# An order of instructions planned by the kernel itself, up to attention's end

## The chip, the cores and the metric

The kernel runs on one core of a Trainium2 chip. The metric is the device time of one execution in microseconds (us); less is better. Five engines each work through a list of instructions in order: PE (matrix products, into PSUM), ACT (functions of one operand), DVE and POOL (elementwise work and reductions) and SP, which here only issues transfers. An instruction waits by semaphores for what it needs, and everything behind it on the same engine waits with it.

## The reference

Attention with normalised queries and keys, then two feed-forward layers over the 1792 tokens. All numbers are float32; the weights come as 64-bit floats, whose two halves the kernel loads and joins itself.

```python
batch, n_heads, seq, head_dim = (4, 12, 448, 64)
q_n, k_n = (rmsnorm(q, g_q), rmsnorm(k, g_k))
scores = scale * np.matmul(q_n, k_n.transpose(0, 1, 3, 2))
scores = scores - np.max(scores, axis=-1, keepdims=True)
attn = np.exp(scores)
attn = attn / (np.sum(attn, axis=-1, keepdims=True) + 1e-09)
x = np.matmul(attn, v)            # then [1792, 768]
h = x @ w_in                      # 768 -> 1024
solu = h * softmax(h)
ln = (solu - mu) / np.sqrt(var + 1e-06) * g_ln
y = ln @ w_out                    # 1024 -> 768
h2 = y @ w2_in                    # 768 -> 2048
out = (h2 - np.tanh(h2)) @ w2_out
```

## The kernel before

Attention runs over 24 pairs of heads, six to a batch. For a pair `load_qk` and `load_v` fetch the data, `norm` scales q and k (squares on ACT, sums `ss` and the root `rr` on DVE and ACT, the product `qn` on POOL), and `qk_trans` transposes them on PE (`qkps`, L276). A matrix is kept as a rounded part and the rest, `wk` and `wq`, which SP copies into one of three large buffers K and Q (`k<-wk`, `q<-wq`). Each pair has two heads, and each head is one "tile" here, 48 in all.

For each tile PE first forms scores for the maxima of the rows (`mps`, L342 and L350), which DVE reduces (`nm`, L351). Four columns of them are transposed (`nmps`, L358), ACT copies the result (`nt`, L360), and SP sends these 2 KB into Q (`q<-nt`, L363), so that the maxima are subtracted by the product itself. Then come the scores (`sps`, L386; for the first pair L380 to L383), their exponential on ACT (`pf`, L395), the product with v (`pvps`, L409), which also gives the sums, and their reading (`sx` and `xu`, L426 and L427). `x_norm` divides (`xo`) and SP stores the result (`xd<-xo`). `mps` and `sps` share three PSUM buffers (`ps_x`), each of which is free when DVE or ACT has read it; `pvps` has two, everything else three (`ps_m`).

The first feed-forward layer runs over blocks of tokens: four blocks of 384, the last with 256 more. As soon as attention has finished a block's tokens, `stage` works on it while later pairs run: `x_split` loads the result back (`xr<-xd`, L504) and splits it on ACT and DVE (`xs`, L195 and L196), `moe_h` multiplies (`hps`), `layer_norm` works on DVE and ACT, `moe_lnT` transposes (`lps`), `moe_x2` multiplies (`x2ps`). Class `Stream` loads weights (`raw`), joins their halves (`val`, L135 to L147), splits them (`w`) and stores them for later blocks (`w_in<-w`, `w_out<-w`). After attention the last block and the second layer (`h2ps`, `ops`) follow.

What is written first is set by two things in the source: a list of attention's steps, sorted by slot (`at`, `step`, `LAG`), of which `attn_next` writes one, and `overlap`, which writes so many of these between the pieces of `stage` as their estimated costs say. The language's own scheduler then places all instructions of the whole program: it simulates the program with its own costs and gives each engine its list, taking what was written earlier first among what its simulation finds ready. SP's list of transfers comes from it too.

Of the kernel before, what the change touches and what calls it, by code (L numbers as in the profile page):

```python
# [8 lines left out]
F32 = mybir.dt.float32  # L9
# [4 lines left out]
AX = mybir.AxisListType  # L14
PSUM = bass.MemoryType.PSUM


@with_exitstack
def kernel(
# [13 lines left out]
):  # L33
    nc = tc.nc
    B, H, S, D = q.shape
# [22 lines left out]

    const = ctx.enter_context(tc.tile_pool(name="const", bufs=1))
    raw_p = ctx.enter_context(tc.tile_pool(name="raw", bufs=2))  # L60
    dram = ctx.enter_context(tc.tile_pool(name="dram", bufs=1, space=bass.MemoryType.DRAM))

    idf = const.tile([128, 128], F32)
    mhalf = const.tile([128, 1], F32)
    eps = const.tile([128, 1], F32)
    tiny = const.tile([128, 1], F32)
    gam = const.tile([128, 1], F32)
    gam2 = const.tile([128, 1], F32)
    gln = const.tile([128, KF1], F32)
    x2d = dram.tile([128, KD, NTOK], F32)  # L70
    xd = dram.tile([128, KD, NTOK], F32)

# [406 lines left out]
    def attn_next():  # L479

        if attn_i[0] < len(attn):
            key = attn[attn_i[0]][0:2]
            while attn_i[0] < len(attn) and attn[attn_i[0]][0:2] == key:
                _, _, _, fn, args = attn[attn_i[0]]
                fn(*args)
                attn_i[0] += 1
            return key
        return (10 ** 6, 0)
# [183 lines left out]
    nc.scalar.preload_act_table_set("natural_log_exp_and_others")  # L672
    make_identity(nc, idf)
    nc.vector.memset(mhalf, -0.5)
    nc.vector.memset(eps, 1e-6)
    nc.vector.memset(tiny, 1e-9)
    ea, eb, ec, ep = ExitStack(), ExitStack(), ExitStack(), ExitStack()
    ps_m = ctx.enter_context(tc.tile_pool(name="ps_m", bufs=3, space=PSUM))
    ps_x = ep.enter_context(tc.tile_pool(name="ps_x", bufs=3, space=PSUM))
    ps_v = ep.enter_context(tc.tile_pool(name="ps_v", bufs=2, space=PSUM))  # L680
    for name, bufs in (
        ("xs", 1), ("xr", 2), ("hb", 3), ("one", 1), ("lnT", 1), ("x2", 2), ("small", 4), ("w", 5),
    ):
        Bp[name] = eb.enter_context(tc.tile_pool(name="b_" + name, bufs=bufs))
    for name, bufs in (
        ("one", 1), ("sq", 2), ("qk", 2), ("vh", 3), ("qt", 1), ("pct", 2),
        ("pc", 6), ("xu", 1), ("xo", 1), ("small", 2),
    ):
        A[name] = ea.enter_context(tc.tile_pool(name="a_" + name, bufs=bufs, side="right"))
    items, w_at = [], {}  # L690
# [9 lines left out]


    attn_next()
    ones = A["qt"].tile([128, 1], F32, tag="ones", name="ones")
# [18 lines left out]
    def overlap(b, batch):  # L722
        left = attn_left(H * (batch + 1) + 3) if batch is not None else 0
        total = stage_cost(b)
        done, spent = 0, 0.0
        for cost in stage(b):
            spent += cost
            while done < left and done < left * spent / total:
                attn_next()
                done += 1  # L730
        while done < left:
            attn_next()
            done += 1

    b = 0
    for batch in range(1, B):
# [3 lines left out]
        overlap(b, batch)  # L740
        b += 1
    ea.close()
    ep.close()
# [4 lines left out]
    def open_c(side, sizes):  # L748
        for name, bufs in sizes:
            C.setdefault(name, []).extend(  # L750
                [ec.enter_context(tc.tile_pool(name=f"c_{name}_{side}{len(C)}", bufs=bufs, side=side))] * bufs
            )

    open_c("right", (("wi", 4), ("wo", 1), ("xh0", 2), ("ob0", 1), ("g", 2), ("th", 2)))
    for name, bufs in (("xs", 1), ("lnT", 1), ("hb", 2)):
        Bp[name + "+"] = eb.enter_context(tc.tile_pool(name=f"b_{name}_2", bufs=bufs, side="right"))
    ps_h = ec.enter_context(tc.tile_pool(name="c_ps_h", bufs=5, space=PSUM))

# [120 lines left out]
```

## Time and profile before

| | |
|---|---|
| time, three runs | 1105.93 us median, 1101.46 to 1106.56 |
| profiled execution, its span from first to last instruction | 1107.5 us |
| PE busy / weight loads | 1043.3 us, 94% / 864.2 us, 78% |
| DVE, ACT, POOL busy | 690.5, 493.1, 236.4 us |
| mean granted PE clock | 0.983 |
| DMA over the span | 171.16 MB, 155 GB/s |

The profiled execution's own time is given only as its span, which lies 1.6 us above the median. Busy shares are means over a first half in which all engines work and a second one in which PE works almost alone. Matmuls are pipelined and the ends of their records are modelled, so that "busy" on PE may hold short gaps. The granted clock is the share of full speed (2.4 GHz) that PE was given; it has two levels, 1.00 and 0.50.

### The profile page before, as it was taken

What the parts mean: (1) busy time and instruction counts of PE and PEld (TensorE: products, weight loads), DVE (VectorE), ACT (ScalarE), POOL (GpSimd) and SP (SyncE); (2) the same over time, 40 slices, a digit from 0 to 9 for tenths busy, and PEclk for the clock granted to TensorE, in tenths of its full rate; (3) what the DMA queues carried; (4) which work ended last, traced back from release to release, by engine and by line L of the source; (5) the groups of instructions that cost most, each with busy time, mean ns of one, the idle gap of its engine ahead of it and who ended that gap; (6) DMA issues with size and microseconds to landing.
All of it is one profiled execution on the core that took longest, in us unless ns stands there. A gap on an engine that the chain in (4) does not pass through costs nothing.

```text
span 1107.5 us, 15169 instructions
## 1 busy us (share of the span) xinstructions
PE 1043.3 (94%) x5348; PEld 864.2 (78%) x5348; DVE 690.5 (62%) x1311; ACT 493.1 (45%) x994; POOL 236.4 (21%) x204
## 2 busy tenths in 40 slices
PE   4989999989887899999999999999999999999998
PEld 2555566648664678778889989898999989898988
DVE  8766686787787453633684066475767666675444
ACT  4667776777677455555255154311212121212110
POOL 2511123121102110001420034242414141322000
PEclk9999999989988999999999999999999999999999
DMA  7987789866996987666786443021112111110004
GB/s 182 274 227 192 179 216 281 207 181 178 284 320 185 327 229 216 192 209 203 227 291 208 138 162 95 23 74 39 57 40 59 55 58 58 57 57 1 1 29 171
DMA packets 113743, 171.16 MB, mean 155 GB/s; under 512 B 31940, under 2 KB 79492, under 8 KB 113668
## 3 DMA queue, kind: packets, MB, share of 16 engines
q1 hardware_dynamic: 112368, 170.20, 52.8%
q8 instruction: 42, 0.69, 0.3%
q14 instruction: 33, 0.27, 0.1%
q10 hardware_dynamic: 1300, 0.01, 0.1%
HBM read 109.32 MB, written 29.10 MB: 125 GB/s over the span
## 4 chain that ended last, share of the span: by engine, by line
PE 72%; DMA 15%; DVE 6%; ACT 4%; issue 1%; SPq 1%; POOL 1%; ACTq 0%; DVEq 0%; POOLq 0%
PE pvps L409 9%; PE ops L191 7%; PE ops L192 7%; PE ops L190 7%; PE h2ps L191 7%; PE h2ps L192 7%; PE h2ps L190 7%; PE sps L386 4%; DMA raw<-in_moe_w_out_dram 3%; PE x2ps L190 3%; PE x2ps L191 3%; PE x2ps L192 3%; DMA q<-nt 2%; DMA raw<-in_moe_w_in_dram 2%; DMA w<-w_in 2%; PE mps L350 1%
## 5 line engine op out<-in xcount | busy, mean ns | idle before, releaser
L820 DVE TENSOR_TENSOR ob<-ops,ob 128x384 f32<-128x384 f32 x196 | 108.5, 554 | 104.1 <-PE ops L192 103.6
L161 POOL TENSOR_TENSOR w<-val,w 128x512 fp32r<-128x512 f32 x60 | 82.5, 1377 | 424.6 <-ACT w L160 397.0
L409 PE MATMUL pvps<-pf,va 128*128 128x448 f32 (+1 forms) x384 | 164.9, 598 | 0.9 <-ACT pf L395 0.9
L191 PE MATMUL ops<-w,gT 128*128 128x384 f32 x448 | 150.6, 336 | 0.0
L190 PE MATMUL ops<-w,gT 128*128 128x384 f32 x448 | 150.3, 336 | 0.0
L192 PE MATMUL ops<-w,gT 128*128 128x384 f32 x448 | 150.2, 335 | 0.0
L351 DVE TENSOR_REDUCE nm<-mps 128x1 f32<-128x448 f32 x168 | 102.6, 617 | 71.1 <-PE mps L350 61.2
L192 PE MATMUL h2ps<-x2s,w 128*128 128x512 f32 (+1 forms) x384 | 140.9, 367 | 0.0
L386 PE MATMUL sps<-q,k 128*128 128x448 f32 (+1 forms) x368 | 118.1, 415 | 24.2 <-DMA q<-nt 9.7
L191 PE MATMUL h2ps<-x2s,w 128*128 128x512 f32 (+1 forms) x384 | 140.9, 367 | 0.0
L190 PE MATMUL h2ps<-x2s,w 128*128 128x512 f32 (+1 forms) x384 | 140.5, 366 | 0.0
L797 ACT ACTIVATE th<-h2ps 128x512 f32<-128x512 f32 (+1 forms) x64 | 34.8, 544 | 182.5 <-PE h2ps L192 182.3
L386 PEld LDWEIGHTS sps<-q,k 128*128 128x128 f32 (+1 forms) x368 | 63.0, 186 | 60.2 <-ACT pf L395 17.6
L395 ACT ACTIVATE pf<-sps 128x448 f32<-128x448 f32 x167 | 88.3, 539 | 38.5 <-PE sps L386 32.5
L409 PEld LDWEIGHTS pvps<-pf,va 128*128 128x128 f32 (+1 forms) x384 | 63.4, 202 | 42.9 <-issue 35.6
L190 PE MATMUL hps<-w,xs 128*128 128x256 f32 (+1 forms) x276 | 90.6, 329 | 2.6 <-DMA w<-w_in 2.6
L266 POOL TENSOR_TENSOR qn<-qk,rr 112x512 f32<-112x512 f32 x44 | 49.0, 1135 | 195.8 <-DVE rr L247 74.7
L350 PE MATMUL mps<-k,q 128*128 128x448 f32 (+1 forms) x144 | 78.4, 553 | 11.1 <-ACT pf L395 3.3
L191 PEld LDWEIGHTS ops<-w,gT 128*128 128x128 f32 x448 | 84.2, 188 | 4.7
L190 PEld LDWEIGHTS ops<-w,gT 128*128 128x128 f32 x448 | 84.2, 188 | 4.4
L192 PE MATMUL hps<-w,xs 128*128 128x256 f32 (+1 forms) x276 | 85.9, 313 | 0.0
L191 PE MATMUL hps<-w,xs 128*128 128x256 f32 (+1 forms) x276 | 85.7, 311 | 0.0
(118 smaller groups left out, 2042.0 us busy)
## 6 DMA issues: line engine op xcount, KB each, us to landing
w<-w_out SPq DMA_DIRECT2D x48, 512.0 KB
raw<-in_moe_w_in_dram SPq DMA_DIRECT2D x36, 512.0 KB
raw<-in_moe_w_out_dram SPq DMA_DIRECT2D x36, 512.0 KB
w<-w_in SPq DMA_DIRECT2D x24, 512.0 KB
k<-wk SPq DMA_DIRECT2D x46, 224.0 KB
q<-wq SPq DMA_DIRECT2D x46, 224.0 KB
w_in<-w SPq DMA_DIRECT2D x12, 512.0 KB
w_out<-w SPq DMA_DIRECT2D x12, 512.0 KB
```

The lines of the kernel that those rows point to most:

```text
L161: nc.gpsimd.tensor_tensor(out=w[:, 1], in0=x, in1=w[:, 0].bitcast(F32), op=ALU.subtract)
L190: nc.tensor.matmul(ps, lhsT=a[0], rhs=w[0], start=first, stop=False)
L191: nc.tensor.matmul(ps, lhsT=a[0], rhs=w[1], start=False, stop=False)
L192: nc.tensor.matmul(ps, lhsT=a[1], rhs=w[0], start=False, stop=last)
L266: eng.tensor_tensor(out=qn[:, a].rearrange("p c h d -> p h c d"), in0=t[:, a], in1=rr[:, a].rearrange("p h (c o) -> p h c o", o=1).to_broa ...
L350: nc.tensor.matmul(ps, lhsT=qh[:, f:f + 128], rhs=kh, start=True, stop=True)
L351: nc.vector.tensor_reduce(out=nm_t[p][:, c:c + 1], in_=ps, axis=AX.X, op=ALU.max, negate=True)
L386: nc.tensor.matmul(o, lhsT=K[p % NQ][:, i, z, k0:k0 + m], rhs=qcols(Q[p % NQ], slice(0, 128), p, i, z), start=(z == 0), stop=(z == 1))
L395: nc.scalar.activation(out=x, in_=ps, func=AF.Exp)
L409: nc.tensor.matmul(pv_t[n], lhsT=w, rhs=pc_t.pop((n, j))[r], start=first, stop=last)
L797: nc.scalar.activation(out=th, in_=ps, func=AF.Tanh)
L820: nc.vector.tensor_tensor(out=o, in0=ps, in1=o, op=ALU.add)
```

## The change

New classes wrap tiles (`View`, `Ref`), pools and engines. From the first step of attention to the end of the last `overlap` that holds attention steps, an instruction is not given to the language but noted, with the parts of buffers that it reads and writes. Then `plan` places them: for each engine it takes, among the noted instructions whose inputs and buffers are free by its reckoning, the one that was written first, at the earliest time; `cost` gives each a duration, `transfer` and the lines on `wire` and `lanes` a time to each DMA. A PSUM tile is opened only when the other inputs of its matmuls are there. `give` hands them out in that order, in a scope in which the language's scheduler keeps the order it gets. From there on the scheduler works as before. `rank`, `lag` and `reserve` have values with which they change no choice. Every noted instruction is issued by one line of `take`, L188, which is why the new pieces all say L188.

```diff
@@ new classes ahead of the kernel @@
+class Pool:
+    def __init__(self, rec, tiles, bufs, psum, name):
+        self.rec, self.tiles, self.bufs, self.psum, self.name = rec, tiles, bufs, psum, name
+
+    def tile(self, shape, dtype, tag=None, name=None):
+        return Ref(self.rec, self, shape, dtype, tag or name, name or tag)
+
+
+class Engine:
+    def __init__(self, rec, name, real):
+        self.rec, self.name, self.real = rec, name, real
+
+    def __getattr__(self, what):
+        f = getattr(self.real, what)
+        if not callable(f):
+            return f
+
+        def call(*a, **kw):
+            self.rec.take(self.name, what, f, a, kw)
+
+        return call
+
+
...
+    def take(self, eng, what, f, a, kw):
+        if not self.on:
+            return f(*[_real(x) for x in a], **{n: _real(x) for n, x in kw.items()})
+        op = Op()
+        op.eng = "dma" if what == "dma_start" else eng
+        op.queue, op.what, op.f, op.a, op.kw = eng, what, f, a, kw
+        op.at, op.rank = len(self.ops), self.rank
+        outs = list(a[:1]) + [kw[n] for n in ("out", "accum_out") if n in kw]
+        ins = list(a[1:]) + [x for n, x in kw.items() if n not in ("out", "accum_out")]
...
+        self.ops.append(op)
+
+    def cost(self, op):
+        n = 1
+        for d in (op.out.shape if isinstance(op.out, View) else [1, 1])[1:]:
+            n *= d
+        src = next((x for x in op.ins if isinstance(x, View)), None)
+        m = n
+        if src is not None:
+            m = 1
+            for d in src.shape[1:]:
+                m *= d
+        big = max(n, m)
+        if op.queue == "tensor":
+            if op.what == "transpose":
+                return (0.095 if n < 128 else 0.108), 0.2
+            rhs = op.kw["rhs"]
+            if rhs.root.dtype != F32:
+                return 0.0025 + n * 0.000451, 0.2
+            return (0.475 if rhs.p1 - rhs.p0 == 64 else 0.75), 0.2
+        if op.eng == "dma":
+            return 0.46, 0.0
...
+        if big <= 16:
+            return 0.18, 0.034
+        slow = isinstance(src, View) and src.dims and abs(src.dims[-1][0]) > 1
+        return 0.156 + 0.00103 * big + (0.1 if slow else 0.0), 0.034
+
+    @staticmethod
+    def transfer(op):
...
+        packets = -(-4 * size // run)
+        return max(1, packets / 16.0) * (8 + 0.05 * run) * 1e-3
+
+    def plan(self):
...
+        def can(op):
+            t = op.ready
+            for r in op.refs:
+                if r.tile_ is not None or r.open:
+                    continue
+                s = slots[r.key]
+                if not s:
+                    return None
+                if opened[r.line] != r.turn or r.wait:
+                    return None
+                t = max(t, r.from_)
+                if r.psum and r.rank and key_limit.get(r.pool.name, 0) >= len(s):
+                    return None
+                t = max(t, min(s))
+            return t
+
+        key_limit = self.reserve
+        while len(order) < total:
+            best = None
+            for e, waiting in ready.items():
+                if not waiting:
+                    continue
+                c = [(can(op), op) for op in waiting]
+                c = [(t, op) for t, op in c if t is not None]
+                if not c:
+                    continue
+                at = max(free[e], min(t for t, _ in c))
+                pick = min((op.rank * self.lag + op.at, op.at, t, op) for t, op in c if t <= at)
+                op = pick[3]
+                start = max(at, op.ready)
+                if best is None or start < best[0]:
+                    best = start, e, op
...
+            start, e, op = best
+            for r in op.refs:
+                if r.tile_ is None and not r.open:
+                    r.open = True
+                    s = slots[r.key]
+                    s.remove(min(s))
+                    opened[r.line] += 1
+            took, late = self.cost(op)
+            if op.eng == "dma":
+                if len(lanes) >= 8:
+                    start = max(start, lanes[-8])
+                free[e] = start + took
+                wire = max(free[e] + 0.4, wire) + self.transfer(op)
+                done = wire + 1.3
+                lanes.append(max(done, lanes[-1] if lanes else 0.0))
+            else:
+                free[e] = start + took
+                done = free[e] + late
+            op.start, op.done = start, done
...
+            for u in users[op.at]:
+                u.left -= 1
+                if u.queue != op.queue or op.eng == "dma":
+                    u.ready = max(u.ready, done + self.notice.get(u.queue, 0.0))
+                else:
+                    u.ready = max(u.ready, start + took)
+                if u.left == 0:
+                    ready[u.queue].append(u)
+        return order
+
+    reserve = {"ps_m": 0}
+    notice = {"tensor": 0.02, "gpsimd": 0.045}
+    lag = 0
+
+    def give(self):
+        order = self.plan()
+        self.on = False
+        with self.tc.manual_schedule():
+            for op in order:
+                self.take(op.queue, op.what, op.f, op.a, op.kw)
+        self.ops = []
 
 
...
-    nc = tc.nc
+    nc = rec = Recorder(tc)
...
+    rec.on = True
     attn_next()
...
         done, spent = 0, 0.0
+        rec.rank = 1
         for cost in stage(b):
             spent += cost
             while done < left and done < left * spent / total:
                 attn_next()
                 done += 1
+        rec.rank = 0
         while done < left:
             attn_next()
...
         overlap(b, batch)
         b += 1
+    rec.give()
     ea.close()
     ep.close()
```

The first place is PE's list in the fifth pair, from the transposed maxima of its first tile (`nmps`) to the first scores of that tile. Before, the scores are the last row (`q_158`; the rows ahead with `q_157` are scores of the tile before, those with 64 rows its tail):

```order
L358 MATMUL nmps<-idf,nm 4x128
L386 MATMUL sps<-q_157,k_154 128x448 x2
L276 MATMUL qkps<-idf,qn 128x112 x4
L350 MATMUL mps<-k_155,q_158 128x448
L386 MATMUL sps<-q_157,k_154 128x448 x2
L350 MATMUL mps<-k_155,q_158 128x448
L386 MATMUL sps<-q_157,k_154 128x448 x2
L386 MATMUL sps<-q_157,k_154 64x448 x2
L386 MATMUL sps<-q_158,k_155 128x448 x2
```

Now, to the last row (`q_170`):

```order
L188 MATMUL nmps<-idf,nm 4x128
L188 MATMUL sps<-q_160,k_184 128x448
L188 MATMUL mps<-k_162,q_170 128x448
L188 MATMUL sps<-q_160,k_184 128x448 x2
L188 MATMUL qkps<-idf,qn 128x112
L188 MATMUL mps<-k_162,q_170 128x448
L188 MATMUL sps<-q_160,k_184 128x448 x2
L188 MATMUL sps<-q_160,k_184 64x448 x2
L188 MATMUL mps<-wk,qd_156 128x448
L188 MATMUL pvps<-pf,va 128x448 x5
L188 MATMUL sps<-q_170,k_162 128x448 x2
```

Five products (`pvps`) and one more `mps` now stand between the two, and three of the four transposes and one `sps` fewer.

The second place is ACT's list at the first block's first `xs`. Before, from the eighth `nt`, behind whose transfer and four others SP's list has the load `xr<-xd`, to `xs` with that load as input:

```order
L360 ACTIVATE nt<-nmps 4x128
L242 ACTIVATE nr<-ss,eps 112x16
L287 ACTIVATE wk<-qkps,gam 128x448
L244 ACTIVATE rr<-nr 112x16
L426 ACTIVATE sx<-pvps,tiny 64x448
L427 ACTIVATE xu<-pvps 64x448
L395 ACTIVATE pf<-sps 128x448
L426 ACTIVATE sx<-pvps,tiny 64x448
L427 ACTIVATE xu<-pvps 64x448
L395 ACTIVATE pf<-sps 128x448
L435 ACTIVATE xo<-sx 128x448
L195 ACTIVATE xs<-xr 128x768
```

Now the eighth `nt` stands 14 rows ahead of these, and behind its transfer and seven others SP's list has the load:

```order
L188 ACTIVATE xo<-sx 128x448
L188 ACTIVATE xo<-xo 128x448
L188 ACTIVATE nt<-nmps 4x128
L188 ACTIVATE pf<-sps 128x448 x2
L188 ACTIVATE wq<-qkps 128x448
L188 ACTIVATE pf<-sps 128x448
L188 ACTIVATE wk<-qkps,gam 128x448
L188 ACTIVATE qd_154<-wq 64x64 x2
L188 ACTIVATE nr<-ss,eps 112x16
L188 ACTIVATE rr<-nr 112x16
L188 ACTIVATE xs<-xr 128x768
```

Between that `nt` and `xs` stand 28 instructions now and 10 before.

## Rows read from the trace of the kernel before

**Rows 1.** The head of the page and its busy times.

```profile
span 1107.5 us, 15169 instructions
PE 1043.3 (94%) x5348; PEld 864.2 (78%) x5348; DVE 690.5 (62%) x1311; ACT 493.1 (45%) x994; POOL 236.4 (21%) x204
```

**Rows 2.** By stretch: us, busy PE, PEld, DVE, ACT, POOL, PEclk, DMA share, GB/s; one group.

```profile
28.00:127.00 99.00, 89.65 (x332) 52.57 (x331) 68.77 (x134) 71.74 (x153) 26.64 (x28) 0.97 0.87 223
127.00:195.00 68.00, 63.26 (x328) 45.29 (x326) 49.28 (x89) 48.17 (x104) 18.61 (x18) 0.97 0.88 236
195.00:410.00 215.00, 188.43 (x925) 137.75 (x925) 157.99 (x336) 144.78 (x319) 34.90 (x36) 0.94 0.84 243
300.00:350.00 50.00, 40.72 (x187) 28.34 (x185) 42.10 (x95) 33.87 (x80) 4.05 (x6) 0.93 0.92 269
514.50:1107.50 593.00, 587.23 (x3165) 537.65 (x3163) 347.26 (x602) 159.59 (x277) 143.73 (x99) 1.00 0.29 92
...
L427 ACT ACTIVATE xu<-pvps x48: 537/538/542, 48.8 to 514.3; 64x448 f32<-64x448 f32 x48
```

**Rows 3.** PE's groups up to 514.5 us: busy, mean ns | idle before, what ended it.

```profile
L386 PE MATMUL sps<-q,k 128*128 128x448 f32 (+1 forms) x368 | 118.1, 415 | 24.2 <-DMA q<-nt 9.7 <-ACT pf L395 9.0 <-DVE nm L351 4.7
L350 PE MATMUL mps<-k,q 128*128 128x448 f32 (+1 forms) x144 | 78.4, 553 | 11.1 <-ACT pf L395 3.3 <-DVE nm L351 3.1 <-DVE nm L575 2.7
L276 PE MATMUL qkps<-idf,qn 112*128 112x112 f32 x192 | 28.7, 275 | 13.4 <-DVE nr L246 11.3 <-DVE qn L266 1.8 <-ACT x L75 0.2
```

**Rows 4.** Timeline (start, us, what, idle before): one q<-nt, and groups with their durations.

```profile
55.17 0.27 PE L358 MATMUL nmps<-idf,nm 128*4 128x128 f32 x1
55.77 0.76 SPq L363 DMA_DIRECT2D q<-nt  x1
62.40 0.47 PE L386 MATMUL sps<-q,k 128*128 128x448 f32 x1 [2.73 <-DMA q<-nt]
...
89.45 1.50 PE L386 MATMUL sps<-q,k 128*128 128x448 f32 x6
120.83 1.67 PE L409 MATMUL pvps<-pf,va 128*128 128x448 f32 x4
```

**Rows 5.** Timeline: xr's load, its reader on ACT, and PE's wait twice.

```profile
80.80 0.58 SPq L504 DMA_DIRECT2D xr<-xd  x1
85.42 0.84 ACT L195 ACTIVATE xs<-xr 128x768 fp32r<-128x768 f32 x1 [2.04 <-DMA xr<-xd]
87.21 0.47 PE L350 MATMUL mps<-k,q 128*128 128x448 f32 x1 [1.32 <-ACT pf L395]
113.88 0.47 PE L350 MATMUL mps<-k,q 128*128 128x448 f32 x1 [1.12 <-ACT pf L395]
```

**Rows 6.** Chain and timeline: a raw weight load, and a load of attention's result, with PE's waits.

```profile
274.18 5.13 DMA raw<-in_moe_w_out_dram
279.40 0.66 ACT L135 ACTIVATE val<-raw 128x512 f32<-128x512 f32 x1 [2.28 <-DVE xo L439]
280.55 0.68 PE L386 MATMUL sps<-q,k 128*128 128x448 f32 x2 [1.91 <-ACT pf L395]
349.21 0.96 DVE L196 TENSOR_TENSOR xs<-xr,xs 128x768 fp32r<-128x768 f32 x1 [3.90 <-ACT xs L195]
350.89 1.11 PE L386 MATMUL sps<-q,k 128*128 128x448 f32 x2 [2.93 <-DVE nm L351]
```

**Rows 7.** Uses of xr with its waits; ACT's group for the raw weights, up to 514.5 us.

```profile
L195 ACT ACTIVATE xs<-xr x13: 622/842/847, 85.4 to 507.1; 128x768 fp32r<-128x768 f32 x11, 128x512 fp32r<-128x512 f32 x2
  DMA xr<-xd: 10.3, 5
...
L135 ACT ACTIVATE val<-raw 128x512 f32<-128x512 f32 x24 | 16.0, 665 | 21.5 <-DMA raw<-in_moe_w_in_dram 9.6 <-DMA raw<-in_moe_w_out_dram 7.5 <-DVE xo L439 2.3
```

**Rows 8.** As rows 2: after the wait at 62.40, and around those at 87 and 113.

```profile
63.30:66.60 3.30, 3.30 (x10) 1.33 (x8) 2.46 (x6) 2.33 (x6) 0.00 (x0) 0.50 0.62 152
84.00:120.00 36.00, 31.93 (x130) 18.87 (x129) 25.32 (x48) 27.89 (x61) 4.91 (x6) 1.00 0.75 186
```

More of the change, by code (lines that the diff above doesn't have):

```diff
@@ new lines, with __init__, get @@
+class Ref(View):
+    def __init__(self, rec, pool, shape, dtype, tag, name):
+        dims, stride = [], 1
+        for n in reversed(shape[1:]):
+            dims.insert(0, (stride, n))
+            stride *= n
+        View.__init__(self, self, [], 0, shape[0], 0, dims)
+        self.rec, self.pool, self.args = rec, pool, (shape, dtype, tag, name)
+        self.dtype, self.tile_ = dtype, None
+        self.key = (pool, tag)
+        self.line = (pool, tag, name if pool.psum else None)
+        self.rank = rec.rank
+        self.psum = pool.psum
+        self.log = []
+        self.open, self.left, self.end = False, 0, 0.0
+        if not rec.on:
+            self.get()
+    def get(self):
+        if self.tile_ is None:
+            shape, dtype, tag, name = self.args
+            self.tile_ = self.pool.tiles.tile(shape, dtype, tag=tag, name=name)
+        return self.tile_
@@ new lines @@
+class Pool:
[3 more added lines that the diff above has]
+        return Ref(self.rec, self, shape, dtype, tag or name, name or tag)
+class Op:
+    pass
+class Engine:
[8 more added lines that the diff above has]
+        return call
@@ L57 @@
     tokens = [sum(n for _, n, _ in b) for b in blocks]
[L59 to L71, printed above, removed]
+    const = rec.tile_pool(ctx, name="const", bufs=1)
+    raw_p = rec.tile_pool(ctx, name="raw", bufs=2)
+    dram = rec.tile_pool(ctx, name="dram", bufs=1, space=bass.MemoryType.DRAM)
+    idf = const.tile([128, 128], F32, name="idf")
+    mhalf = const.tile([128, 1], F32, name="mhalf")
+    eps = const.tile([128, 1], F32, name="eps")
+    tiny = const.tile([128, 1], F32, name="tiny")
+    gam = const.tile([128, 1], F32, name="gam")
+    gam2 = const.tile([128, 1], F32, name="gam2")
+    gln = const.tile([128, KF1], F32, name="gln")
+    x2d = dram.tile([128, KD, NTOK], F32, name="x2d")
+    xd = dram.tile([128, KD, NTOK], F32, name="xd")
     def copy(eng, out, in_, **kw):
@@ L484, in attn_next @@
                 _, _, _, fn, args = attn[attn_i[0]]
+                was, rec.rank = rec.rank, 0
                 fn(*args)
+                rec.rank = was
                 attn_i[0] += 1
@@ L672 @@
     nc.scalar.preload_act_table_set("natural_log_exp_and_others")
-    make_identity(nc, idf)
+    make_identity(nc.nc, idf.real)
     nc.vector.memset(mhalf, -0.5)
@@ L677 @@
     ea, eb, ec, ep = ExitStack(), ExitStack(), ExitStack(), ExitStack()
-    ps_m = ctx.enter_context(tc.tile_pool(name="ps_m", bufs=3, space=PSUM))
-    ps_x = ep.enter_context(tc.tile_pool(name="ps_x", bufs=3, space=PSUM))
-    ps_v = ep.enter_context(tc.tile_pool(name="ps_v", bufs=2, space=PSUM))
+    ps_m = rec.tile_pool(ctx, name="ps_m", bufs=3, space=PSUM)
+    ps_x = rec.tile_pool(ep, name="ps_x", bufs=3, space=PSUM)
+    ps_v = rec.tile_pool(ep, name="ps_v", bufs=2, space=PSUM)
     for name, bufs in (
@@ L683 @@
     ):
-        Bp[name] = eb.enter_context(tc.tile_pool(name="b_" + name, bufs=bufs))
+        Bp[name] = rec.tile_pool(eb, name="b_" + name, bufs=bufs)
     for name, bufs in (
@@ L688 @@
     ):
-        A[name] = ea.enter_context(tc.tile_pool(name="a_" + name, bufs=bufs, side="right"))
+        A[name] = rec.tile_pool(ea, name="a_" + name, bufs=bufs, side="right")
     items, w_at = [], {}
@@ L755 @@
     for name, bufs in (("xs", 1), ("lnT", 1), ("hb", 2)):
-        Bp[name + "+"] = eb.enter_context(tc.tile_pool(name=f"b_{name}_2", bufs=bufs, side="right"))
-    ps_h = ec.enter_context(tc.tile_pool(name="c_ps_h", bufs=5, space=PSUM))
+        Bp[name + "+"] = rec.tile_pool(eb, name=f"b_{name}_2", bufs=bufs, side="right")
+    ps_h = rec.tile_pool(ec, name="c_ps_h", bufs=5, space=PSUM)
     def next_w(kind, i):
```

214 lines of the change are left out of this document (213 added, 1 removed).

## Prediction

> **What bounds the kernel now.** I read the page's head first, then busy time and granted clock by stretch, then PE's costliest groups with what ended their idle time, then single places on the timeline. The head shows a span of 1107.5 us with PE busy 94% [rows 1]. The stretches show that this is an average over two halves. The last product of attention ends at 514.3 + 0.54 = 514.8 us [rows 2]. From 514.5 us to the end PE is busy 587.2 of 593.0 us at full clock: there is nothing to win there. Before that, the three stretches from 28 to 410 us have granted clocks of 0.97, 0.97 and 0.94, and DMA engines that are busy 0.87, 0.88 and 0.84 of the time [rows 2]. PE looks 88 to 93% busy there, but overlapping ends of pipelined matmuls hide short gaps, so I count its waits instead.
>
> The groups show them up to 514.5 us: the score matmuls (sps) stood 24.2 us, 9.7 of it for the small transfer q<-nt, 9.0 for an exponential (ACT pf) and 4.7 for a row maximum (DVE nm); the maxima matmuls (mps) stood 11.1 us, 3.3 for pf, 3.1 for nm and 2.7 for a layer-norm maximum (L575); the transposes (qkps) stood 13.4 us, of which 11.3 is the one wait at the start of the program [rows 3]. So some 37 us of visible waits after the start, and on top the clock: (1 - 0.97) x 99 + (1 - 0.97) x 68 + (1 - 0.94) x 215 = 3.0 + 2.0 + 12.9 = 17.9 us, the time that half-rate stretches cost at most, if PE alone set the pace. Together 55 us are in reach.
>
> **What the change does to each.** No computation is added or taken away: what changes up to 514.8 us is the order on each engine and on SP's queue. After attention's last product the order on PE is as before, but for eight transposes (lps) that now stand ahead of it; so the 593 us are carried over unchanged, and every term below belongs to the first 514.8 us.
>
> *Waits for q<-nt, 10 us.* Four maxima are transposed (nmps), copied by ACT (nt) and sent by SP into Q before the first sps of their tile may run. One case: nmps at 55.17, the DMA issued at 55.77, and the sps starts at 62.40 after 2.73 us of idle PE [rows 4]. Between the two, PE has in the order before eight sps, two mps and four qkps (first pair of order pieces). By the durations of such groups (1.50 us for six sps, 1.67 for four records of pvps, which are two products, 28.7 / 192 = 0.15 for a qkps [rows 3, 4]) that is 10 x 0.25 + 4 x 0.15 = 3.1 us of work to cover a transfer that took over 6. In the new order seven sps, three mps, one qkps and five products stand there: 10 x 0.25 + 0.14 + 5 x 0.83 = 6.8 us. The short piece stands at nine of the 24 even tiles before; in the new order at two. The longest wait is 2.7 us, less than the 3.7 by which the piece grows, so where it grows the wait goes. Two of eight waits stay (the first one of the program and one near 244 us), and some are partly covered: I take 7 us, bounds 3 and 10.
>
> *Instructions that wait for a big DMA at the head of ACT or DVE, 7 us on PE.* The load xr<-xd is issued at 80.80; ACT reaches xs at 85.42 after 2.04 us of idling, the exponentials queued behind it come late, so no score buffer is free, and PE's mps stands 1.32 us [rows 5]. The same again costs 1.12 us at 113.88. At 279.40 ACT stands for a raw weight load of 5.13 us (the row names another releaser, the chain has the load's landing right ahead of it; PE then loses 1.91), at 349.21 DVE stands 3.90 us for xs with the maxima behind it (PE loses 2.93) [rows 5, 6]. That is 1.32 + 1.12 + 1.91 + 2.93 = 7.3 us of PE. On ACT the waits of this kind sum to 10.3 us for xs and 17.1 for val [rows 7]. The new order puts the first xs 28 ACT instructions behind the nt that precedes its load on SP, where 10 stood (second pair of pieces: before the whole stretch, now its end); both of the first two xs have that, the third has less than before. I take 6, bounds -4 (if third and later ones fare worse) and 7.
>
> *Waits for nm and pf that come from the order of short instructions, 15 us.* 9.0 + 3.3 less the 4.35 above, and 4.7 + 3.1 + 2.7 less 2.93, leave 15.5 us [rows 3]. All maxima and scores share three PSUM buffers, each free only when DVE or ACT has read it. The new order has fewer runs of four or more such tiles in a row on PE (15 instead of 21), but more of three (26 instead of 14). A long layer-norm or weight instruction ahead of nm stays possible. I take 2, bounds -8 (half again as many) and 8 (half of them).
>
> *The start.* The first weight conversions stood among the first maxima on DVE and now stand behind them; the 11.3 us to the first transpose stay [rows 3]. 1 us, bounds 0 and 2.
>
> *POOL and SP.* Every transfer and every qn moves with the rest. POOL has room for it (26.6 busy of 99 us, 34.9 of 215 [rows 2]), and the waits of qkps after the start sum to 2.1 us [rows 3], so the products reach PE in time now; from the third pair on the new order has the transposes of a pair further ahead of its maxima than before. On SP a transfer that waits holds up those behind it; what that costs is in the nt and xs terms. 0 us, bounds -3 and 2.
>
> *The clock.* Half rate follows a wait: after the 2.73 us that end at 62.40, the stretch from 63.3 to 66.6 runs at 0.50, that is 1.2 of 2.4 GHz [rows 4, 8]. The terms above remove 7 + 6 + 2 = 15 of 37 us of waits, 40%, so 40% of 17.9 comes back: 7 us, bounds -5 and 15.
>
> Sum: 7 + 6 + 2 + 1 + 0 + 7 = 23 us; attention ends near 492, and the span is 1084.5. The span profiled lies 1107.5 - 1105.9 = 1.6 us above the median of the runs, which I take off: 1083 us. What is late next are the DMA engines: from 28 to 410 us they are busy 0.87 x 99 + 0.88 x 68 + 0.84 x 215 = 326.6 us of 382. In 359 us that would be a share of 0.91; the stretch from 300 to 350 already shows 0.92 [rows 2]. So the engines allow this gain, but hardly twice as much.
>
> **A rule that speaks against the clock term.** In the trace each half-rate stretch that I looked at stands behind one long wait; the waits of 1.3 and 1.1 us at 87 and 114 us have none, the clock is at 1.00 around them [rows 5, 8]. The Trainium skill, page TensorE: Matmul & The Clock Gate, section "A second HAM failure mode: psum-queue depth-cycling", says that cycling through PSUM banks can also make the clock swing, by many small idles between groups and no long one. By that rule the more frequent runs of three tiles would cost clock even though long waits go; the trace so far bears it out weakly. It is the third rival.
>
> **Rivals.** (1) *Slower: the list's landings are too early for the loaded engines.* An order given out in advance is only as good as its transfer times. ACT has 13 xs and 24 val before attention's end; they wait 10.3 + 17.1 = 27.4 us today [rows 7], and PE loses 7.3 us by it, 0.27 us per us. If they wait two and a half times as long, 41 us more, PE loses 11 more, and 5 of clock in the same measure as now (17.9 / 37 = 0.48 us per us of waiting): 16 us; the nt gain of 7 shrinks to 2. 1106 + 16 - 2 = 1120 us. It decides from the point at which a load takes longer than the ACT work behind which its reader stands; against it speaks the second pair of pieces, for it the third xs and a DMA share near 0.9. (2) *No change: the DMA engines take the gain back.* If 0.88, the highest of the three stretches, is all that the order can get out of them, 326.6 / 0.88 = 371 us, 11 less than 382; with half of it lost to new waits, 1100. For it: landings of 4.6 and 5.1 us in rows 5 and 6; against it: 0.92 over 50 us. (3) *Less: the clock doesn't come back.* The waits go as forecast but 0.94 holds from 28 to 410 us: 0.06 x 382 = 22.9, 5 more than now instead of 7 less: 1083 + 12 = 1095. (4) *More: nearly all waits go.* 37 - 5 of the waits and 14 of the clock: 1106 - 46 = 1060; beyond it the DMA engines would need 326.6 / 336 = 0.97.
>
> **How the numbers follow.** A difference of 0.5%, 5.5 us, is about what a measurement of this kernel can tell from no change. Chances: the forecast, 1070 to 1090, 0.42; more, below 1070, 0.16; less (3), 1090 to 1100, 0.10; no change, 1100.4 to 1111.5, 0.12; slower, 0.20. Faster is 0.42 + 0.16 + 0.10 = 0.68. The likeliest has its own range of 1070 to 1090. For eight in ten I leave out the lower end of the larger gain, below 1054, and the slower cases beyond 1116.
>
> **What would show it.** The first stretches: xu's last start near 491 instead of 514.3, and the remaining time still 593 us. PE's sps waits for q<-nt under 4 us; ACT's first two xs without a wait for xr; granted clock from 195 us on at 0.96 or more; DMA share up to 0.87 or more in the same stretch. I am wrong if ACT's waits for raw and xr grow, if mps and sps wait longer for nm and pf than the 20.1 us of now (4.7 + 9.0 + 3.3 + 3.1), or if the part after attention gets longer.

## The result, and the profile after

The changed kernel took 1120.57 us (median of 4 runs, 1119.65 to 1122.37) against 1105.53 for the kernel before on the same chip: a ratio of 1.014, 95% interval 1.011 to 1.0171. It is 15 us slower, where I had forecast 23 us less. The head of the page and its busy times, to hold against [rows 1]:

```profile
span 1118.0 us, 15156 instructions
PE 1051.1 (94%) x5348; PEld 872.7 (78%) x5348; DVE 703.6 (63%) x1311; ACT 497.9 (45%) x994; POOL 239.7 (21%) x204
```

The stretches of [rows 2], with the same columns, with one for the start ahead of them, and then xu's group with its first and last start:

```profile
28.00:50.00 22.00, 22.00 (x57) 13.68 (x57) 9.46 (x19) 8.85 (x19) 3.15 (x4) 1.00 0.45 111
28.00:127.00 99.00, 90.62 (x317) 53.54 (x317) 75.56 (x135) 70.98 (x150) 27.77 (x26) 0.98 0.80 211
127.00:195.00 68.00, 63.55 (x318) 45.05 (x316) 47.30 (x88) 47.99 (x101) 18.11 (x18) 0.97 0.87 228
195.00:410.00 215.00, 189.19 (x927) 142.43 (x926) 162.01 (x336) 144.89 (x316) 36.57 (x37) 0.91 0.89 250
```

```profile
L188 ACT ACTIVATE xu<-pvps x48: 537/538/543, 53.6 to 527.2; 64x448 f32<-64x448 f32 x48
```

The two profiled executions differ by 10.5 us of span. Attention ends at 527.2 + 0.5 = 527.7 us instead of 514.8, and the rest takes 1118.0 - 527.7 = 590.3 us, not longer than the 593 of before. All of the loss lies in attention. PE's busy time doesn't show where: 22.00 of 22 us at the start, 189 of 215 later.

The groups of PE's waits up to 514.5 us (total, times, longest) are these:

```profile
PE qkps L188 <- DVE qn L188: 12.6, 3, 11.7
PE sps L188 <- DMA q<-nt: 11.1, 9, 2.5
PE sps L188 <- ACT pf L188: 7.1, 8, 2.8
PE qkps L188 <- ACT nt L188: 5.0, 3, 4.4
PE nmps L188 <- DVE wk L188: 4.9, 1, 4.9
PE mps L188 <- DVE nm L188: 4.0, 7, 1.3
...
PE mps L188 <- ACT pf L188: 2.5, 4, 1.8
PE sps L188 <- DVE nm L188: 2.4, 3, 1.8
```

The waits don't explain 13 us. All rows of this view, the small ones included, sum to 61.5 us, against 57.4 before. Those of sps and mps for nm and pf are 7.1 + 4.0 + 2.5 + 2.4 = 16.0 us, less than the 20.1 of before [rows 3], and those for q<-nt are 11.1 us, against 10.3 (the 9.7 of [rows 3] and 0.6 in the first pair, L383).

The first thing that differs is the start. First PE's timeline of the changed kernel, then of the kernel before:

```profile
34.13 1.86 PE L188 MATMUL sps<-q,k 64*128 64x448 f32 x4
35.92 0.74 PE L188 MATMUL mps<-k,q 128*128 128x448 f32 x1
...
48.70 5.21 PE L188 MATMUL pvps<-pf,va 128*128 128x448 f32 x12
```

```profile
28.38 1.86 PE L409 MATMUL pvps<-pf,va 128*128 128x448 f32 x2
...
33.03 0.36 PE L381 MATMUL sps<-q,k 64*128 64x448 f32 x1
33.23 0.37 PE L382 MATMUL sps<-q,k 64*128 64x448 f32 x1
33.44 0.36 PE L383 MATMUL sps<-q,k 64*128 64x448 f32 x1
```

Before, the first product with v runs at 28.38, and from 33 us on score products follow each other every 0.20 us. Now the first product runs at 48.70, twelve records or six products in a row, and until then four score products take 1.86 us. The trace's first record of the clock is its rise: at 32.5 us before, at 50.5 now. Ahead of the first record the table prints 1.00, which is no measurement. PE was busy all the time from 28 to 50 us, at half rate: its score products follow each other every 0.37 us there, and run 5 below has a record of 0.50 over this stretch.

The start isn't where the loss stays, though. These are PE's records (matmuls, in parentheses) from 0 to 50, 250, 350 and 490 us, with the share of the clock, DMA share and GB/s, before and then now:

```profile
0.00:50.00 50.00, 32.52 (x101) 1.00 0.89 224
0.00:250.00 250.00, 212.68 (x908) 0.97 0.83 215
0.00:350.00 350.00, 300.63 (x1374) 0.96 0.85 226
0.00:490.00 490.00, 431.54 (x2069) 0.96 0.83 228
```

```profile
0.00:50.00 50.00, 32.44 (x86) 1.00 0.61 148
0.00:250.00 250.00, 215.24 (x911) 0.98 0.82 215
0.00:350.00 350.00, 296.20 (x1335) 0.95 0.83 225
0.00:490.00 490.00, 430.44 (x2036) 0.95 0.82 224
```

At 50 us the changed kernel is 15 records behind, at 250 us it is level, and from there to 350 us it falls behind again. So two things are to be explained: what the late start takes away, and what happens between 250 us and the end of attention.

The waits of ACT up to 514.5 us show a line that the kernel before doesn't have, and one that shrank from 10.3 [rows 7]:

```profile
ACT pf L188 <- PE pvps L188: 11.3, 8, 3.9
...
ACT xs L188 <- DMA xr<-xd: 4.7, 1, 4.7
```

An exponential waits for a product: its buffers are full, because products come late. The late first product and this wait point to one rule of the plan, "a PSUM tile is opened only when the other inputs of its matmuls are there". The tile of a pair's first head collects four products, the last of them over the score tile that both heads share. By the rule none of the four may run before that shared tile's exponential.

### The profile page after: what moved, and what is told of

Same layout as the page of the kernel before. It is cut to its first block, busy times and chain, and to the rows that moved or that the text cites. A ratio compares the mean times of both kernels' runs of the same rounds, so it can differ in the third digit from the quotient of the medians.

```text
span 1118.0 us, 15156 instructions
## 1 busy us (share of the span) xinstructions
PE 1051.1 (94%) x5348; PEld 872.7 (78%) x5348; DVE 703.6 (63%) x1311; ACT 497.9 (45%) x994; POOL 239.7 (21%) x204
## 4 chain that ended last, share of the span: by engine, by line
PE 69%; DMA 4%; DVE 2%; ACT 1%; issue 1%; SPq 0%; POOL 0%; ACTq 0%; DVEq 0%; POOLq 0%
PE ops L188 21%; PE h2ps L188 21%; PE x2ps L188 9%; PE hps L188 7%; PE pvps L188 5%; PE sps L188 3%; DMA q<-nt 1%; DMA q<-wq 1%; PE lps L188 1%; DMA raw<-in_moe_w_in_dram 1%; DMA w<-w_out 1%; PE mps L188 1%; DMA raw<-in_moe_w_out_dram 0%; DVE lnT L188 0%; DVE val L188 0%
## 5 line engine op out<-in xcount | busy, mean ns | idle before, releaser
L188 PE MATMUL h2ps<-x2s,w 128*128 128x512 f32 (+1 forms) x1152 | 259.4, 367 | 0.0
L188 PE MATMUL ops<-w,gT 128*128 128x384 f32 x1344 | 257.5, 336 | 0.0
L188 PEld LDWEIGHTS ops<-w,gT 128*128 128x128 f32 x1344 | 235.8, 188 | 9.0
L188 PEld LDWEIGHTS h2ps<-x2s,w 128*128 128x128 f32 x1152 | 200.1, 188 | 30.1
L188 DVE SCALAR_TENSOR_TENSOR val<-raw,val 128x512 int32<-128x512 int32 (+1 forms) x192 | 149.7, 782 | 71.0 <-POOL val L188 67.9
L188 DVE TENSOR_TENSOR ob<-ops,ob 128x384 f32<-128x384 f32 x196 | 108.6, 555 | 103.8 <-PE ops L188 103.3
L188 POOL TENSOR_TENSOR w<-val,w 128x512 fp32r<-128x512 f32 x60 | 82.2, 1373 | 409.4 <-ACT w L188 402.7
L188 PE MATMUL sps<-q,k 128*128 128x448 f32 (+3 forms) x400 | 136.9, 444 | 20.7 <-DMA q<-nt 11.1
L188 PE MATMUL pvps<-pf,va 128*128 128x448 f32 (+1 forms) x384 | 152.9, 571 | 0.0
L188 DVE TENSOR_REDUCE nm<-mps 128x1 f32<-128x448 f32 x168 | 100.4, 619 | 74.5 <-PE mps L188 73.6
L188 PE MATMUL hps<-w,xs 128*128 128x256 f32 (+1 forms) x828 | 135.4, 317 | 2.1 <-DMA w<-w_in 2.1
L188 PEld LDWEIGHTS hps<-w,xs 128*128 128x128 f32 x828 | 121.4, 196 | 15.4 <-issue 3.7
L188 PE MATMUL x2ps<-lnT,w 128*128 128x384 f32 (+1 forms) x720 | 123.8, 328 | 0.6 <-DMA w<-w_out 0.4
L188 PEld LDWEIGHTS x2ps<-lnT,w 128*128 128x128 f32 x720 | 117.7, 188 | 4.3 <-issue 2.4
L188 ACT ACTIVATE th<-h2ps 128x512 f32<-128x512 f32 (+1 forms) x64 | 34.8, 544 | 182.4 <-PE h2ps L188 182.2
L188 PEld LDWEIGHTS sps<-q,k 128*128 128x128 f32 (+3 forms) x400 | 74.0, 204 | 53.8 <-DMA q<-nt 13.3
L188 ACT ACTIVATE pf<-sps 128x448 f32<-128x448 f32 (+1 forms) x169 | 89.8, 540 | 57.5 <-PE sps L188 43.8
L188 PEld LDWEIGHTS pvps<-pf,va 128*128 128x128 f32 (+1 forms) x384 | 61.4, 195 | 49.6 <-issue 43.6
L188 POOL TENSOR_TENSOR qn<-qk,rr 112x512 f32<-112x512 f32 x44 | 51.6, 1192 | 188.6 <-DVE rr L188 47.2
L188 POOL TENSOR_SCALAR val<-raw 128x512 f32<-128x512 f32 x48 | 79.3, 1654 | 28.0 <-DMA raw<-in_moe_w_out_dram 11.8
L188 ACT ACTIVATE gT<-th 128x512 fp32r<-128x512 f32 (+1 forms) x64 | 37.0, 579 | 98.9 <-PE ops L188 67.0
L188 PE MATMUL mps<-k,q 128*128 128x448 f32 (+1 forms) x144 | 67.3, 498 | 9.7 <-DVE val L188 3.0
```

The source lines that it names most:

```text
L188: return f(*[_real(x) for x in a], **{n: _real(x) for n, x in kw.items()})
```

## Experiments

Theory A: the rule brings the products late, which leaves the clock down at the start and the buffers full later. Theory B: the plan reckons with transfers that land too early (the last instruction that it places is done at 475.8 us by its reckoning). Ratios are to the kernel before, measured alongside on the same chip; their 95% intervals stand in parentheses.

**1. The products' tiles exempt from the rule.**

```diff
-                    if r not in o.refs:
+                    if r not in o.refs and r.pool.name != "ps_v":
```

> The changed kernel, except that the rule 'open a PSUM tile only when the other inputs of its matmuls are there' no longer holds for the tiles of the products (pvps). Theory A (late products: by that rule all products of a pair's first head stand behind the exponential of the shared last score tile, so PE has no product until 48.7 us, the clock rises only at 50.5 us, and later ACT waits 11.3 us for pf buffers): the first product starts before 32 us, the clock rises before 36 us, ACT's waits pf<-pvps fall under 4 us, and the time falls by 8 to 16 us, to 1105 to 1112. Theory B (the landings of DMAs are planned too early, and that is what stretches 476 planned us to 527): the products come earlier as well, but the time stays within 4 us of 1120.6.

1111.45 us, ratio 1.0035 (1.0005 to 1.0065): 1.05% of the 1.4% comes back. ACT's wait for pf<-pvps is gone. In the profiled execution, which has 9.4 us of this gain, the first product started only at 33.7 and the clock rose at 47.5 us, 3 us earlier than in the changed kernel. So little of the gain came by way of the clock at the start; from 195 to 410 us the granted clock was 0.94 again instead of 0.91. PE's waits for q<-nt grew:

```profile
PE sps L188 <- DMA q<-nt: 18.9, 13, 3.0
```

**2. Landings planned 1 us later.** `done = wire + 1.3` becomes `wire + 2.3`.

> The changed kernel, planned with 2.3 us instead of 1.3 us between a transfer's end on the wire and its landing; nothing else. Theory A (late products): the order of the products stays late, the time stays within 4 us of 1120.6. Theory B (landings planned too early): readers move further behind their loads, PE's waits for q<-nt fall from 11.1 to under 6 us, ACT's and DVE's waits for loads fall, and the time falls by 6 to 15 us, to 1106 to 1115.

1126.55 us, 1.018 (1.0123 to 1.0236), which overlaps with the changed kernel's interval. PE's waits for q<-nt were 9.9 us, hardly less than 11.1. As long as the products are late, planning this much later gains nothing.

**3 and 4. The rule's effect in the kernel before**, for the first pair and for all pairs (`True` in place of `p == 0`):

```diff
-        first, last = (j == 0, j == 3) if i == 0 else (j == 3, j == 2)
+        first, last = (j == 0, j == 3) if i == 0 and not (p == 0) else (j == 3, j == 2)
...
-                step(z + LAG + 4 + j, pv, n, j)
+                step(4 * s + LAG + 8 if i == 0 and (p == 0) else z + LAG + 4 + j, pv, n, j)
```

> The kernel before, with the products of the first head of the first pair behind that pair's shared last score tile (the tile of the product then starts with that part), as the rule of the plan has it; the other 23 pairs as before. Theory A in its form for the clock (without products the clock stays at its lower level at the start): the first product starts after 40 us instead of 28.4, the clock rises about 2 to 4 us behind it instead of at 32.5, and the time grows by 4 to 9 us, to 1110 to 1115. If the late rise of the clock costs nothing in the end (the other engines set the pace up to 50 us, or the lost work is caught up by 250 us as the changed kernel's was): within 3 us of 1105.5.

1112.78 us, 1.0062 (1.0041 to 1.0083). The first product came at 49.4 us, the clock rose at 49.6. One pair's order costs 7 us. ACT has no wait of pf for pvps there, so it is not the full buffers that cost.

> The kernel before, with the products of the first head of every pair behind the pair's shared last score tile. Theory A (the late products are what costs in the changed kernel): slower than before by 10 to 20 us, 1115 to 1126, with waits of ACT for pf buffers (pf<-pvps) that the kernel before doesn't have. Theory B (landings): the late products cost little where the language's scheduler sets the order, at most 5 us, so 1110 or less.

1134.88 us, 1.0249 (1.0205 to 1.0294), more than expected, and the full buffers appear as a wait of ACT:

```profile
ACT pf L395 <- PE pvps L409: 22.3, 14, 3.1
```

Theory A's part on the products holds without any list: late products alone cost up to 28 us.

**5 to 7. Five products of zeros at the start of PE's list**, in the changed kernel, in that of run 1, and in the kernel before:

```diff
+    warm = const.tile([128, 512], F32, name="warm")
+    nc.vector.memset(warm, 0.0)
+    wps = ps_m.tile([128, 512], F32, tag="m", name="wps")
+    for z in range(5):
+        nc.tensor.matmul(wps, lhsT=warm[:, :128], rhs=warm, start=(z == 0), stop=(z == 4))
```

> The changed kernel with five products of a tile of zeros (128x512, their result is never read) at the very start of PE's list, where PE has nothing to do for 11.7 us; the list is otherwise unchanged. Theory A, its part on the clock (PE runs at the lower of its two levels until 50.5 us, because it has done too little before): the clock rises before 15 us, the alternation of scores and maxima from 27 to 48 us takes 6 to 9 us less, and the time falls by 4 to 9 us, to 1112 to 1117. If the clock falls again in PE's waits between 12 and 25 us, or if ACT and DVE set the pace up to 50 us anyway: within 3 us of 1120.6.

1122.67 us, 1.0141 (1.0082 to 1.0201): nothing. The stretches show why; the clock now has a record ahead of 50 us:

```profile
6.20:13.00 6.80, 3.63 (x14) 1.57 (x13) 5.75 (x18) 4.01 (x12) 0.27 (x1) 1.00 0.69 131
13.20:50.00 36.80, 30.66 (x78) 18.29 (x79) 21.57 (x46) 15.45 (x34) 5.38 (x6) 0.50 0.61 153
50.80:60.00 9.20, 8.76 (x40) 5.62 (x39) 8.20 (x13) 6.58 (x13) 4.54 (x4) 1.00 0.69 213
```

The clock rose at 6.1 us, fell at 13.0 in PE's next waits and stayed at 0.50, 1.2 of 2.4 GHz, until 50.5 us. This run doesn't test what the cold start costs, but it measures that PE was at half rate there.

> Both: the tiles of the products exempt from the rule, and the five products of zeros at the start. Theory A, with its two parts adding up: 4 to 9 us under the kernel with the exemption alone (1111.5), that is 1102 to 1108. If the exemption had already given back what the cold start costs: within 3 us of 1111.5.

1106.50 us, 1.0001 (0.9965 to 1.0036): the interval overlaps with that of run 1, and the clock was down from 13.0 to 47.2 us. Inconclusive.

> The kernel before with the same five products of zeros at the start of PE's list. There the clock rises at 32.5 us, so theory A gives less to win than in the changed kernel: 2 to 6 us, 1100 to 1104; nothing within 2 us if the wait for data sets the pace up to 32 us.

1114.12 us, 1.0072 (1.003 to 1.0113): slower. The clock was down from 12.2 to 39.5 us, where the kernel before has it up at 32.5. The scheduler also moved some of PE's instructions (a maxima and four score products now stand behind the first product, where four transposes stood), so the 7 us can't be put down to the clock alone.

**8. Products' tiles exempt, and 3.0 us for landings.**

> The changed kernel with the tiles of the products exempt from the rule, and planned with 3.0 us instead of 1.3 us between a transfer's end on the wire and its landing. Theory B in its second form (what is left once the products come in time, above all 18.9 us of PE's waits for q<-nt, comes from landings that are planned too early): those waits fall under 10 us and the time falls by 5 us or more against the exemption alone, to 1106 or less. Against it stands the run with 2.3 us, which was slower than the changed kernel: by that, 1111 or more.

1096.06 us, 0.9916 (0.9881 to 0.995): faster than both kernels, and 1.2% under run 1. The clock rose at 34.7 us, and the waits for q<-nt are a third of those of run 1:

```profile
PE sps L188 <- DMA q<-nt: 6.4, 4, 2.8
```

**9. The changed kernel's list, with PE kept at work until 30 us.** The planned order stays; products of zeros fill PE's planned gaps up to the first real product, with ten more ahead of the first scores that wait for q<-nt.

```diff
+                        many = int((op.start - end) / 0.2)
...
+                        for _ in range(many):
+                            self.filler()
```

> The changed kernel with the list as it is, and products of a tile of zeros (128x448, their result is never read) put into PE's planned gaps up to 27 us: 37 ahead of the first transpose, some 50 between the first maxima and scores. With five products at the start alone the clock rose at 6.1 us and fell again at 13.0, in PE's next waits, until 50.5; here PE has no such waits. Theory A, its part on the clock: the clock stays up from some 10 us on, the stretch from 27 to 48 us takes 6 to 10 us less, and the time falls by 4 to 9 us against the changed kernel, to 1112 to 1117. If the stretch up to 50 us is set by ACT and DVE, or if what is won there is lost again behind it: within 3 us of 1121.

1111.67 us, 1.0036 (1.0004 to 1.0067): 1.04% comes back from work whose result nobody reads; PE's order of real instructions is that of the changed kernel. One stretch, and two rows of the timeline:

```profile
28.00:50.00 22.00, 22.00 (x95) 14.16 (x95) 17.11 (x30) 13.18 (x29) 8.03 (x8) 1.00 0.67 175
```

```profile
33.87 1.07 PE L188 MATMUL sps<-q,k 64*128 64x448 f32 x4
...
42.09 4.33 PE L188 MATMUL pvps<-pf,va 128*128 128x448 f32 x12
```

The clock was up from 6.3 to 88.2 us. In the 22 us in which the changed kernel's PE worked through 57 records, "busy" throughout, it now works through 95, of which the first ten are products of zeros. Four score products take 1.07 instead of 1.86 us, the first product comes 6.6 us earlier, the first xu 7.5 us earlier, and attention ends at 517.9 instead of 527.7: what the start gives is still there at the end.

**10 and 11. The 3.0 us only for transfers sent in the plan's first 60 us, and only behind them.**

```diff
-                done = wire + 1.3
+                done = wire + (3.0 if wire < 60.0 else 1.3)
```

> Products' tiles exempt from the rule; the landing counted with 3.0 us only for transfers that the plan sends in its first 60 us, with 1.3 us behind that. The run with 3.0 us throughout took 1096, the one with 1.3 us throughout 1111.5, and two thirds of the difference in PE's work stood by 100 us (its clock rose at 34.7 us, the other's at 47.5). Theory A, clock at the start: 1097 to 1103. Theory B, landings all along: 1106 to 1111.

1104.03 us, 0.9943 (0.9914 to 0.9972).

> The reverse: the landing counted with 1.3 us in the plan's first 60 us, with 3.0 us behind that. Up to 60 us the list is that of the kernel with the exemption alone, so the clock should rise at about 47 us again. Theory A, clock at the start: 1106 to 1111. Theory B, landings all along: PE's waits for q<-nt fall from 18.9 to under 10 us, and the time is 1097 to 1103.

1106.82 us, 0.9988 (0.9954 to 1.0023). Against 1.0035 without either and 0.9916 with both, the early part is worth some 0.8%, the late part some 0.4%. The early part counts; the late one is at the edge of what these intervals can tell. In run 11 PE's waits for q<-nt fell to 9.5 us, as theory B had it, and the time stayed in theory A's range. Theory A's reason, the clock at the start, isn't shown by it, since the list doesn't fix the clock: runs 8 and 10 have the same list for the plan's first 60 us, and the clock rose at 34.7 us in one profiled execution and at 47.9 in the other; runs 1 and 11 likewise, at 47.5 and 34.9.

**12. Runs 8 and 9 together.**

> Products' tiles exempt, 3.0 us for every landing, and the products of zeros in PE's planned gaps up to the first real product. If the cold start still costs there (the clock rose at 34.7 us, so from 12 to 34 us PE runs at the lower level, much of it waiting): 2 to 5 us under the 1096 without them. If PE waits for data there and not the reverse: within 2 us of 1096.

1096.19 us, 0.988 (0.9832 to 0.9927), as fast as run 8 within the intervals: on this list the products of zeros give nothing that can be told from noise.

**13. Runs 1 and 9 together.**

> The changed kernel with both edits that gave back 9 us each: products of zeros in PE's planned gaps up to the first real product, and the products' tiles exempt from the rule; landings at 1.3 us as in the changed kernel. If the cold start and the late products are two causes: 1101 to 1105. If they are one cause seen twice: 1109 to 1113.

1105.10 us, 0.9971 (0.9948 to 0.9995). By ratios 1.69% under the changed kernel, where the two alone gave 1.05 and 1.04: two causes that add up for the most part. In microseconds it lies 0.1 us outside the first range.

**14. As 13, every transfer 15% longer on the wire, the feed-forward stages ranked 400 places later.**

```diff
-        return max(1, packets / 16.0) * (8 + 0.05 * run) * 1e-3
+        return max(1, packets / 16.0) * (8 + 0.05 * run) * 1.15e-3
...
-    lag = 0
+    lag = 400
```

> As the run before, and planned with every transfer 15% longer on the wire (landing still 1.3 us), and with the feed-forward stages' instructions ranked as if written 400 places later, so that attention's go first. Theory B in its second form (once products come in time, longer planned transfers pay): 1085 to 1096, as with 3.0 us of landing or better. If 3.0 us was a lucky list and not a cause: 1100 to 1107.

1098.29 us, 0.9918 (0.989 to 0.9946). The time lies between the two ranges. A second list that is planned for slower transfers beats the 1.3 us of run 13, which speaks against 3.0 us being a lucky list; it doesn't show it, because the rank of the stages was changed at the same time. Attention ended at 469.0 us, 35 us earlier than in run 12, and the kernel was no faster: the rest took 1096.2 - 469.0 = 627.2 us, because the stages' work had moved behind it.

## Why the prediction was wrong

**The step that failed first is the start**: "1 us, bounds 0 and 2", as a gain. It cost: the first xu comes at 53.6 instead of 48.8 us, 4.8 us later than before, and run 9 gives back 1.04% of 1106, 11.5 us (7 to 16 by the two intervals), by keeping PE at work and the clock up there, with the list as it is. I had read the clock from 28 us on as 0.97 [rows 2]; its record begins at 32.5 us, and nothing in my sum asked what PE did before, or what would delay the rise. The products stood in my own working: "five products" behind an nmps, counted as 4.15 us of cover for q<-nt. I did not ask why five stand together. They had been held back by the rule that the section on the change quotes.

**The sum counted only waits that go, and took new ones for nothing.** By the trace its terms came out roughly so, against the kernel before: start -5 us, q<-nt -1, big transfers -8, nm and pf +4, clock -6. That is -16 where the sum had +23, and attention ended 13 us later (some waits count twice). So the terms on big transfers and on the clock missed by more than the start did; they are taken up below.

**Late products later on**: no term and no rival had them. Run 13 against run 9 puts them at 0.65%, 7 us.

**Waits for q<-nt, "I take 7 us"**: they grew, from 10.3 to 11.1 us. I compared the work between the transposed maxima and the scores; the transfer itself moved too. One case, where the maxima are transposed at 342.63, ACT stands for the store of a weight, and SP sends the maxima at 351.08, behind six other transfers:

```profile
342.63 0.27 PE L188 MATMUL nmps<-idf,nm 128*4 128x128 f32 x1
...
344.79 1.28 ACT L188 ACTIVATE w<-val,gln 128x128 fp32r<-128x128 f32 x4 [4.42 <-DMA w_out<-w]
...
347.42 0.25 ACT L188 ACTIVATE nt<-nmps 4x128 fp32r<-4x128 f32 x1
...
347.67 1.73 PE L188 MATMUL qkps<-idf,qn 112*128 112x112 f32 x8 [4.37 <-ACT nt L188]
...
351.08 0.65 SPq L188 DMA_DIRECT2D q<-nt  x1
```

That the plan's landings matter for these waits is shown by runs 1 and 8 (18.9 to 6.4 us); the changed kernel itself, with its late products, did not gain from later landings (run 2).

**Instructions that wait for a big transfer, 6 us**: right on ACT (xs 10.3 to 4.7 us; val's waits for raw, 17.1, are now 5.0), but PE got nothing of it. The places moved: besides the 4.37 us above, PE stood 3.04 us at 289.84, where on ACT eight pieces of a weight (2.43 us) and a val that waited 0.45 us for its load stood ahead of pf, 4.86 at 316.45, where weights stood ahead of wk on DVE, and 2.78 at 497.37 behind the eleventh of ACT's 13 xs ("if third and later ones fare worse"):

```profile
285.82 2.43 ACT L188 ACTIVATE w<-val,gln 128x128 fp32r<-128x128 f32 x8
...
288.69 0.66 ACT L188 ACTIVATE val<-raw 128x512 f32<-128x512 f32 x1 [0.45 <-DMA raw<-in_moe_w_out_dram]
...
289.84 0.74 PE L188 MATMUL mps<-k,q 128*128 128x448 f32 x1 [3.04 <-DVE val L188]
...
316.45 0.27 PE L188 MATMUL nmps<-idf,nm 128*4 128x128 f32 x1 [4.86 <-DVE wk L188]
...
495.67 0.84 ACT L188 ACTIVATE xs<-xr 128x768 fp32r<-128x768 f32 x1 [4.67 <-DMA xr<-xd]
...
497.37 0.94 PE L188 MATMUL sps<-q,k 128*128 128x448 f32 x2 [2.78 <-ACT pf L188]
```

These four are 15.1 us of PE, twice the 7.3 that I had seen go. The last is a wait for a load and the one at 347.67 for the store of a weight; at the other two long weight work stands in the way. What each is worth was not tried one by one.

**Waits for nm and pf, 2 us**: they fell by 4 us, inside the bounds (by 6.8, if layer norm's 2.7 of before, which the changed kernel's rows hold under the same name, is counted).

**The clock, 7 us back**: wrong in sign. From 195 to 410 us it is 0.91 instead of 0.94, 6.5 us more lost by the form of my own sum. Half-rate stretches begin at 289.4, 316.7, 347.4 and 497.6 us, each within 0.5 us of the end of one of the four waits above, and the four others up to 515 us (from 118.7, 146.0, 241.6 and 255.3) within 0.8 us of the end of waits of 1.8 to 2.5 us, so "half rate follows a wait" held; the longest, in the columns of [rows 2]:

```profile
347.50:361.00 13.50, 10.51 (x25) 5.99 (x26) 13.23 (x33) 6.76 (x14) 3.58 (x3) 0.50 0.95 282
```

The sign came from counting only the waits that go. What this trace doesn't need there is the rule of the Trainium skill, page TensorE: Matmul & The Clock Gate, section "A second HAM failure mode: psum-queue depth-cycling", that many small idles between groups cost clock. Whether it bears on the start this trace can't tell: from 28 to 50 us PE alternates scores and maxima without an idle record, and the clock doesn't swing but stays at half rate.

**The part after attention**: right, 590.3 for 593 us. **The rivals**: the slower one's 1120 us was met for the most part by a mechanism that it didn't have. Its heading, landings planned too early, was right for one part (0.9%, run 12 against 13), but not its path: ACT's waits for raw and xr, by which I would have known it, shrank.

**What is left of the idea.** A planned order can gain: run 8 stands at 0.9916 without any products of zeros. Runs 12 and 13 against 9 take away the late products (0.65%) and the early landings (0.9%), and 12 stands at 0.988. The late start, the late products and the early landings together cost 2.6% and turned 1.2% faster into 1.4% slower. Which of the later waits each of them moves stays open, as does how far the second layer's instructions that the language's scheduler puts into the same lists disturb them (the plan has no val of POOL; one at 343.59 us held DVE for 3.79 us).

## What to carry to other kernels

A PE that is "busy" is not one that works at full rate: look at the distance of equal matmuls, above all ahead of the first record of the clock. When an order is made by rules, follow one accumulating tile through them: a rule that waits for all inputs delays the first product to the last input. Where a plan reckons with landings, try later ones (here 3.0 us beat 1.3, once the products came in time), and judge by the span, not by the end of the stage that was planned.

## What the runs showed of the hardware

The clock's rise is not fixed by the list: with the same instructions on PE it came 13 us apart (34.7 and 47.9, 34.9 and 47.5 us). The products do bear on it: in the five traces in which the first comes at 45.9 to 49.4 us (the changed kernel, runs 2 to 5) the last rise of the start came at 47.5 to 50.5, in the seven without filled gaps in which it comes at 27.5 to 33.7 us, at 32.5 to 47.9. Whether the spread of the runs comes from it is open: run 8 spread over 13 us in 10 runs, run 12, where PE is kept at work, over 2.6 us in 4, but run 9, where it is too, over 12 us in 10. Products of zeros raise the clock too (in run 5 at 6.1 us); it fell again at 13.0, in waits soon after, and stayed down for 37.5 us.
